# Inverse lengths by logarithm on ScalarE, unscaled maxima and value products in pieces in the first stage of an attention and maxout kernel

## The chip, the cores and the metric

The kernel runs on one core of one Trainium2 chip. A core has five engines that matter here: TensorE (matrix products, into PSUM), VectorE, ScalarE, GpSimd and SyncE (SP, which issues most of the transfers). Each engine works through its own instructions in the order in which the program gives them, and waits on semaphores for the others. The metric is the device time of one execution in microseconds; the kernel before takes 1111.87 us, the median of 3 runs (1109.64 to 1112.04).

## The reference

For 8 batches and 12 heads, queries and keys of 448 rows x 64 are divided by their root mean square and multiplied with gains; then softmax attention; the 12 heads' outputs of a row make a row of 768, which goes through three 768 x 768 layers, the largest of the three at each place, and a last 768 x 768 layer.

```python
def rmsnorm(x, g):
    rms = np.sqrt(np.mean(x * x, axis=-1, keepdims=True) + 1e-06)
    return x / rms * g
q_n, k_n = (rmsnorm(q, g_q), rmsnorm(k, g_k))
scores = np.matmul(q_n, k_n.transpose(0, 1, 3, 2)) / np.sqrt(64)
scores = scores - np.max(scores, axis=-1, keepdims=True)
attn = np.exp(scores)
attn = attn / (np.sum(attn, axis=-1, keepdims=True) + 1e-09)
attn_out = np.matmul(attn, v)
h = np.maximum(np.maximum(x @ w1, x @ w2), x @ w3)
out = h @ w_out
```

All inputs are float32. (The scale is written in one line here.)

## The kernel before

Two heads of a batch make a **pair**; there are 48 pairs, `g` = 0 to 47. Every pair is worked in 12 **beats** (`beat(g, i)`, `i` = 0 to 11), and a pair's 448 queries in four quarters `c` of 112, three beats each. The order of every engine is written out by hand: what a beat calls is recorded in the order of the calls, and `later(n, work)` puts work n beats on, to the end of that beat (`tick`). So an engine's order is the beats' order, and an engine can run ahead of another by some beats until it waits.

The work of one quarter: `scores` (TensorE), `row_max` (VectorE, the negative maximum, L550), `softmax` (ScalarE: L558 scales the maxima with `down`, L567 takes the exponential of `down * score + nm` for each of two heads). In the first six pairs (`PLAIN` = 6) scores and value products are float32 products; the exponentials `e` are transposed on TensorE (`turn_plain`), copied by ScalarE (`keep_turned`, L599, `pt`), and multiplied with the values in one go of eight products in beat 4 of the next pair (`add_values`, L680, into the only `av` buffer). The exponentials' sums are inverted, spread over the partitions (beat 5), copied (`keep_sums`, ScalarE, beat 6) and multiplied in (`scale_plain`, VectorE, beat 8); `finish` splits the result into two float16 parts `xt`: ScalarE the upper one in beat 9 (L705), VectorE the lower one a beat later (L706). From the seventh pair on everything is in two float16 parts and three products.

A pair's queries and keys are made ready two pairs ahead: squares (`squares`, GpSimd, L363; ScalarE for the first two pairs), their sums (VectorE, L370), mean and power -0.5 (`inv_rms`, GpSimd, L381 and L385, for keys and queries apart), scaling (`scale_k`, `scale_q`, GpSimd; VectorE for pair 0). In the plain pairs keys and queries are turned on TensorE (`turn_whole`, L461) and copied by ScalarE (`keep_whole`, L473 for keys, L475 for queries with the column of gains `gain_c`).

Beside the first pairs runs the preparation of the weights, in 24 blocks: a transfer (`raw`, L221, two buffers), ScalarE (L186), three decoding steps on VectorE (L194, L198, L203), a largest value over three blocks (L168), and then a split in two float16 parts: ScalarE L266 and L267, and GpSimd L270 for the lower part. The last one is called a weight piece below. From the seventh pair on the layers' products (L720, L784) fill TensorE between the attention's own, a few per beat (`thirds`).

The transfers of keys, queries, values and weights all stand in SP's one queue; a key load waits there until the scaling has freed its buffer.

## Time and profile before

| | |
|---|---|
| median of 3 runs | 1111.87 us (1109.64 to 1112.04) |
| the profiled execution | 1110.84 us; span of its records 1109.0 us |
| TensorE, VectorE, ScalarE, GpSimd busy | 1017.1, 755.3, 771.2, 702.4 us |
| mean granted TensorE clock | 0.967 |
| GpSimd's powers (L385) | 96 of 1603 ns, 153.9 us |
| scaling of the maxima (L558) | 192 of 265 ns, 50.9 us |
| exponentials (L567) of the plain pairs | 48 of 720 ns |

Busy time is that of an engine in all stages together; the plain pairs take the first 145 us or so, and in the rest TensorE is nearly full. A wait is told as the engine that idled, the line that it idled before, and the line that released it. In a timeline a row gives the start, the length, the engine, line, operation, what is written and read, and in brackets the idle time just before and what ended it.

### The profile page before, as it was taken

Reading aid. Unit: us, or ns where it says so; the run is one execution under the profiler, and the core shown is the slowest. Engines: PE = TensorE matmul, PEld = TensorE weight load, DVE = VectorE, ACT = ScalarE, POOL = GpSimd, SP = SyncE. Lnnn points to the kernel's source line nnn. Section 1 sums busy time; section 2 is a strip of 40 time slices with the busy share of each in tenths; the row PEclk is TensorE's granted clock in tenths of the full one; section 3 lists DMA queues with packets and bytes.
Section 4 is the critical chain, followed back from the end, with each engine's and each line's share of the span. In section 5 each row is a group of like instructions: output and inputs, shape, how many; then the busy total and the mean of one; then the engine's idle time right before and its main releaser. Section 6 shows DMA issues by size and latency. Waiting matters only on the chain. (4 is left out here: it accounts for less than half of the span.)

```text
span 1109.0 us, 18435 instructions
## 1 busy us (share of the span) xinstructions
PE 1017.1 (92%) x6184; PEld 500.3 (45%) x6184; DVE 755.3 (68%) x1397; ACT 771.2 (70%) x1767; POOL 702.4 (63%) x805
## 2 busy tenths in 40 slices
PE   4668759887899999999999999999999999999998
PEld 2334334343444444444444444444444444445554
DVE  4799988887667676776677766777677666662210
ACT  4599888767777687777777777777777777773001
POOL 5478888775767767677677675776767767610000
PEclk9697879998999999999999999999999999999999
DMA  5554567955888779777887798777877788564002
GB/s 150 161 164 151 139 175 142 188 118 102 172 147 147 134 153 179 152 142 139 170 149 143 143 164 173 144 137 154 169 142 139 140 173 154 91 106 87 1 1 57
DMA packets 426494, 152.30 MB, mean 137 GB/s; under 512 B 372896, under 2 KB 422048, under 8 KB 426400
## 3 DMA queue, kind: packets, MB, share of 16 engines
q1 hardware_dynamic: 425888, 150.95, 67.4%
q8 instruction: 49, 0.80, 0.3%
q14 instruction: 45, 0.37, 0.1%
q10 hardware_dynamic: 512, 0.18, 0.1%
HBM read 51.97 MB, written 11.01 MB: 57 GB/s over the span
## 5 line engine op out<-in xcount | busy, mean ns | idle before, releaser
L720 PE MATMUL acc<-xt,w_sb 128*128 128x448 f16 x2592 | 515.5, 354 | 2.7 <-DVE ht L744 2.2
L720 PEld LDWEIGHTS <-w_sb 128*128 128x128 f16 x2592 | 244.1, 98 | 260.8 <-issue 48.3
L550 DVE TENSOR_REDUCE sc<-sc 112x2 f32<-112x896 f32 x192 | 209.6, 1092 | 53.3 <-PE sc L541 52.2
L567 ACT ACTIVATE sc<-sc,nm,down 112x448 f32<-112x448 f32 x336 | 234.4, 698 | 11.2
L643 ACT ACTIVATE pp<-sc,rs 112x448 f16<-112x448 f32 x336 | 195.0, 633 | 52.0 <-ACT sc L567 47.4
L653 DVE SCALAR_TENSOR_TENSOR pp<-sc,rs,pp 112x448 f16<-112x448 f32 x336 | 212.9, 675 | 4.4 <-ACT pp L643 3.9
L784 PE MATMUL acc<-wo_sb,ht 128*128 128x384 f16 x864 | 151.9, 328 | 12.0 <-ACT osb L793 7.3
L558 ACT ACTIVATE nm<-sc,down 112x2 f32<-112x2 f32 x192 | 50.9, 265 | 158.2 <-DVE sc L550 157.7
L385 POOL TENSOR_TENSOR ri<-ri,half_neg 128x7 f32<-128x7 f32 x96 | 153.9, 1603 | 8.0
L541 PE MATMUL sc<-kt,qt 64*112 64x448 f16 x1008 | 132.1, 367 | 21.5 <-DVE pp L653 18.6
L749 POOL COPY hx<-ht 128x128 f16<-128x128 f16 x48 | 16.2, 337 | 168.0 <-DVE ht L744 167.6
L784 PEld LDWEIGHTS <-ht 128*128 128x128 f16 x864 | 81.4, 98 | 79.4 <-issue 29.0
L691 PE MATMUL av<-pt,vp 128*64 128x448 f16 x1008 | 109.9, 359 | 0.0
L541 PEld LDWEIGHTS <-qt 64*112 64x112 f16 x1008 | 54.2, 126 | 91.6 <-issue 52.4
L438 POOL TENSOR_TENSOR kp<-kn,kp 128x512 f16<-128x512 f32 x42 | 50.5, 1202 | 67.1 <-ACT kp L432 67.1
L636 DVE TENSOR_SCALAR rs<-sc 112x2 f32<-112x2 f32 x168 | 26.7, 159 | 91.1 <-ACT sc L567 91.0
L519 POOL TENSOR_TENSOR vp<-vr,vp 128x448 f16<-128x448 f32 x42 | 44.5, 1059 | 63.0 <-ACT vp L513 61.3
L691 PEld LDWEIGHTS <-vp 128*64 128x64 f16 x1008 | 50.1, 109 | 54.7 <-issue 29.5
L706 DVE SCALAR_TENSOR_TENSOR xt<-av,xt 128x448 f16<-128x448 f32 x42 | 26.2, 625 | 67.0 <-ACT xt L705 67.0
L370 DVE TENSOR_REDUCE ss<-sq 128x7 f32<-128x448 f32 x96 | 61.0, 637 | 10.4 <-ACT sq L361 6.4
L438 POOL TENSOR_TENSOR qp<-qn,qp 112x512 f16<-112x512 f32 x42 | 48.6, 1156 | 19.2 <-ACT qp L432 19.2
L505 POOL TENSOR_SCALAR vr<-vr,v_up 128x448 f32<-128x448 f32 x42 | 60.4, 1438 | 0.0
(111 smaller groups left out, 1202.6 us busy)
## 6 DMA issues: line engine op xcount, KB each, us to landing
raw<-in_moe_w_dram SPq DMA_DIRECT2D x18, 768.0 KB, 4.3
qr<-in_q_dram SPq DMA_DIRECT2D x48, 224.0 KB, 2.8
vr<-in_v_dram SPq DMA_DIRECT2D x96, 96.0 KB, 2.5
kr<-in_k_dram SPq DMA_DIRECT2D x95, 96.0 KB, 3.0
raw<-in_moe_w_out_dram SPq DMA_DIRECT2D x6, 768.0 KB, 5.1
pt<-pp SPq DMA_TRANSPOSE x168, 4.0
out_dram<-osb SPq DMA_DIRECT2D x8, 336.0 KB, 3.0
out_dram<-osb SPq DMA_DIRECT2D x8, 288.0 KB, 3.6
```

What stands on the lines that cost most here:

```text
L370: nc.vector.tensor_reduce(sums[g % 2][:sq.shape[0], KQ[what]], sq, axis=AX, op=ALU.add)
L385: nc.gpsimd.tensor_tensor(out=ri, in0=ri, in1=half_neg[:, at], op=ALU.pow)
L438: nc.gpsimd.tensor_tensor(out=parts[:, 1], in0=n, in1=parts[:, 0], op=ALU.subtract)
L505: nc.gpsimd.tensor_scalar(out=vr, in0=vr, scalar1=v_up[:, g // NP:g // NP + 1], scalar2=None, op0=ALU.mult,)
L541: nc.tensor.matmul(sc[:QP, h, :S], qt[rows, qp, c], kt[rows, kp, KEYS[h]], start=n == 0, stop=n == len(TERMS) - 1,)
L550: nc.vector.tensor_reduce(sc[:QP, 0, S + 8:S + 10], sc[:QP, :, :S], axis=AX, op=ALU.max, negate=True)
L567: nc.scalar.activation(to, sc[:QP, h, :S], AF.Exp, bias=nm[:, h:h + 1], scale=down[:QP], accum_out=total,)
L643: nc.scalar.activation(pp[:, 0, h], sc[:QP, h, :S], AF.Copy, scale=rs[:, h:h + 1])
L653: nc.vector.scalar_tensor_tensor(out=pp[:, 1, h], in0=sc[:QP, h, :S], scalar=rs[:, h:h + 1], in1=pp[:, 0, h], op0=ALU.mult, op1=ALU.subtract,)
L691: nc.tensor.matmul(av[half, :S], vp[rows, group, vpart], pt[rows, 7 * wp + group], start=u == 0 and n == 0, stop=u == 3 and n == len(TERMS ...
L720: nc.tensor.matmul(acc[:, :S], wt[:, wp, c], xs[c][:, xp], start=(c == 0 and n == 0), stop=(c == NCT - 1 and n == 2),)
L784: nc.tensor.matmul(acc[:, :HW], lhs, wo_sb[:, f, wp, half * HW:(half + 1) * HW], start=(f == 0 and n == 0), stop=(f == NFT - 1 and n == 2),)
```

## The change

Five things change.

- The power -0.5 of the mean squares is the exponential of -0.5 times the logarithm, two ScalarE operations on 128 x 15 for keys and queries together (`power`), followed by one Newton step (`newton`): four small GpSimd operations, three VectorE ones for the first two pairs. The mean is one operation (`mean_squares`, GpSimd; VectorE for the first two pairs). One table set for both functions is loaded at the start.
- The first pair's gains are worked later; `gain_c` holds the whole scale of the plain pairs' scores. So in the plain pairs `row_max` writes `nm` itself, and `softmax` has no scaling of the maxima there.
- Squares stand in beats 0 and 1 (before 0 and 3), their sums in 2 and 3 (before 2 and 5), the mean in 4, the power in 6, the Newton step and the keys' scaling in 8. Pair 1's scaling and turning are put later.
- For the first five pairs the value products come in four pieces in beats 2, 4, 5 and 7; spreading, copying and multiplying in of the sums in 8, 9 and 10 (before 5, 6, 8), `finish` in beat 11 (before 9).
- The order at the start is written anew: sums, mean and power for keys and queries together, then the keys, the gains' product, the queries.

```diff
+    nc.scalar.preload_act_table_set("natural_log_exp_and_others")
     nc.scalar.activation(warm, warm, AF.Exp)
...
-    def inv_rms(g, what):
...
-        nc.gpsimd.tensor_scalar(
-            out=ri, in0=sums[g % 2][:, at], scalar1=1.0 / D / QK_UP ** 2,
+    def mean_squares(g):
+        s = st[g]
+        s["ms"] = sb.tile([P, 15], F32, name="ms", bufs=2)
+        (nc.gpsimd if g > 1 else nc.vector).tensor_scalar(
+            out=s["ms"], in0=sums[g % 2], scalar1=1.0 / D / QK_UP ** 2,
             scalar2=RMS_EPS / QK_UP ** 2, op0=ALU.mult, op1=ALU.add,
         )
-        nc.gpsimd.tensor_tensor(out=ri, in0=ri, in1=half_neg[:, at], op=ALU.pow)
+    def power(g):
+        s = st[g]
+        ri = sb.tile([P, 15], F32, name="ri", bufs=2)
+        nc.scalar.activation(ri, s["ms"], AF.Ln)
+        nc.scalar.activation(ri, ri, AF.Exp, scale=-0.5)
+        s["ri"] = ri.rearrange("p (n o) -> p n o", o=1)
+    def newton(g):
+        s = st[g]
+        ms, ri = s.pop("ms"), s["ri"][:, :, 0]
+        t = sb.tile([P, 15], F32, name="newton", bufs=2)
+        if g > 1:
+            nc.gpsimd.tensor_tensor(out=t, in0=ms, in1=ri, op=ALU.mult)
+            nc.gpsimd.tensor_tensor(out=t, in0=t, in1=ri, op=ALU.mult)
+            nc.gpsimd.tensor_scalar(
+                out=t, in0=t, scalar1=-0.5, scalar2=1.5, op0=ALU.mult, op1=ALU.add
+            )
+            nc.gpsimd.tensor_tensor(out=ri, in0=ri, in1=t, op=ALU.mult)
+            return
...
     def row_max(g, c):
...
+        to = sc[:QP, 0, S + 8:S + 10]
+        if g < PLAIN:
+            to = s["nm", c] = sb.tile([QP, 2], F32, name="nm", bufs=3)
+        nc.vector.tensor_reduce(to, sc[:QP, :, :S], axis=AX, op=ALU.max, negate=True)
     def softmax(g, c):
...
-        nm = sb.tile([QP, 2], F32, name="nm", bufs=3)
-        nc.scalar.activation(nm, sc[:QP, 0, S + 8:S + 10], AF.Copy, scale=down[:QP])
         if g < PLAIN:
...
+            nm, by = s.pop(("nm", c)), 1.0
+        else:
+            nm, by = sb.tile([QP, 2], F32, name="nm", bufs=3), down[:QP]
+            nc.scalar.activation(nm, sc[:QP, 0, S + 8:S + 10], AF.Copy, scale=by)
...
-    sum_squares(0, "k")
-    inv_rms(0, "k")
-    sum_squares(0, "q")
-    inv_rms(0, "q")
-    prep_gain()
+        sum_squares(0, what)
+    mean_squares(0)
+    power(0)
+    newton(0)
     scale_k(0)
+    nc.vector.tensor_tensor(out=gain, in0=gains[:, 0], in1=gains[:, 1], op=ALU.mult)
     scale_q(0)
...
-    nc.scalar.copy(gain_c, column[:, 0:1])
+    nc.scalar.activation(
+        gain_c, column[:, 0:1], AF.Copy, scale=1.0 / QK_UP ** 2 / float(D) ** 0.5
+    )
...
-        inv_rms(1, what)
-    scale_k(1)
-    scale_q(1)
+    mean_squares(1)
+    later(0, lambda: power(1))
+    later(1, lambda: newton(1))
+    later(1, lambda: scale_k(1))
+    later(1, lambda: scale_q(1))
+    later(4, prep_gain)
...
-            if i == 5:
+            last = w == PLAIN - 1
+            if i == (5 if last else 8):
                 spread_sums(w)
-            if i == 6:
+            if i == (6 if last else 9):
                 keep_sums(w)
-            if i == (8 if w < PLAIN else 9):
+            if i == (8 if last else 10):
                 scale_plain(w)
-        if w >= 0 and i == (4 if w < PLAIN else 7):
+        if 0 <= w < PLAIN - 1 and i in (2, 4, 5, 7):
+            add_values(w, [(2, 4, 5, 7).index(i)])
+        elif w >= PLAIN - 1 and i == (4 if w < PLAIN else 7):
             add_values(w)
...
-        if w >= 0 and i == (9 if w < PLAIN else 10):
+        if w >= 0 and i == (11 if w < PLAIN - 1 else 9 if w < PLAIN else 10):
             finish(w, x_of[w // NP])
...
-                if i in (1, 4):
+                at = i - (1 if g else 4)
+                if at in (0, 3):
...
-            if i in (0, 3):
-                squares(n, "kq"[i // 3])
-            if i in (2, 5):
-                sum_squares(n, "kq"[i // 3])
-            if i in (5, 7):
-                inv_rms(n, "kq"[i // 7])
+            if i in (0, 1):
+                squares(n, "kq"[i])
+            if i in (2, 3):
+                sum_squares(n, "kq"[i - 2])
+            if i == 4:
+                mean_squares(n)
+            if i == 6:
+                power(n)
             if i == 8:
+                newton(n)
                 scale_k(n)
```

The lines of the changed kernel have other numbers, up to 30 apart. **VectorE, end of plain pair 2 and start of pair 3**, before: `xt` is the attention's lower part, the `sc` rows are the maxima, `w_sb` the decoding, `most` the largest of a block row.

```order
L706 SCALAR_TENSOR_TENSOR xt<-av,v_up,xt 128x448
L550 TENSOR_REDUCE sc<-sc 112x2
L194 TENSOR_SCALAR w_sb<-raw 128x768
L257 TENSOR_SCALAR w_most<-most 128x1
L260 RECIPROCAL w_up<-w_most 128x1
L261 TENSOR_SCALAR w_up<-w_up 128x1
L198 SCALAR_TENSOR_TENSOR w_sb<-raw,w_sb 128x768
L203 SCALAR_TENSOR_TENSOR w_sb<-raw,w_sb 128x768
L550 TENSOR_REDUCE sc<-sc 112x2
L611 RECIPROCAL sum<-sum 112x8
L370 TENSOR_REDUCE ss_84<-sq 128x7
L168 TENSOR_REDUCE most<-w_sb 128x1
```

The same place after:

```order
L256 TENSOR_SCALAR w_most<-most 128x1
L259 RECIPROCAL w_up<-w_most 128x1
L260 TENSOR_SCALAR w_up<-w_up 128x1
L735 SCALAR_TENSOR_TENSOR xt<-av,v_up,xt 128x448
L197 SCALAR_TENSOR_TENSOR w_sb<-raw,w_sb 128x768
L202 SCALAR_TENSOR_TENSOR w_sb<-raw,w_sb 128x768
L578 TENSOR_REDUCE nm<-sc 112x2
L639 RECIPROCAL sum<-sum 112x8
L369 TENSOR_REDUCE ss_83<-sq 128x7
L167 TENSOR_REDUCE most<-w_sb 128x1
L369 TENSOR_REDUCE ss_83<-sq 112x8
L193 TENSOR_SCALAR w_sb<-raw 128x768
```

`xt` has moved behind the next pair's first maximum and the first decoding step; the query sums (`ss`, 112x8) have moved from behind the third maximum to ahead of it.

**GpSimd, beats 0 to 8 of a plain pair**, before: `w_sb` is a weight piece, `sq` the query squares, `ri` the mean and the power for keys and then for queries.

```order
L270 TENSOR_TENSOR w_sb<-w_sb 128x768
L363 TENSOR_TENSOR sq<-qr 112x512
L270 TENSOR_TENSOR w_sb<-w_sb 128x768
L381 TENSOR_SCALAR ri<-ss_85 128x7
L385 TENSOR_TENSOR ri<-ri,half_neg 128x7
L381 TENSOR_SCALAR ri<-ss_85 128x8
L385 TENSOR_TENSOR ri<-ri,half_neg 128x8
```

After:

```order
L269 TENSOR_TENSOR w_sb<-w_sb 128x768
L362 TENSOR_TENSOR sq<-qr 112x512
L376 TENSOR_SCALAR ms<-ss_84 128x15
L269 TENSOR_TENSOR w_sb<-w_sb 128x768
L395 TENSOR_TENSOR newton<-ms,ri 128x15
L396 TENSOR_TENSOR newton<-newton,ri 128x15
L397 TENSOR_SCALAR newton<-newton 128x15
L400 TENSOR_TENSOR ri<-ri,newton 128x15
```

The mean now stands ahead of the second weight piece, and the Newton step behind it.

More of the change, by code (lines that the diff above doesn't have):

```diff
@@ L130, in qknorm_attention_maxout_ffn_kernel @@
     nc.vector.memset(warm, 0.0)
+    nc.scalar.preload_act_table_set("natural_log_exp_and_others")
     nc.scalar.activation(warm, warm, AF.Exp)
-    half_neg = const.tile([P, 15], F32, name="half_neg")
-    nc.vector.memset(half_neg, -0.5)
     sums = [const.tile([P, 15], F32, name=f"ss{i}") for i in range(2)]
@@ L666, in turn_weights, with add_values @@
         )
-    def add_values(g):
+    def add_values(g, groups=range(4)):
         s = st[g]
-        av = ps_a.tile([P, 512], F32, name="av", tag="a")
-        s["av"] = av
+        if "av" not in s:
+            s["av"] = ps_a.tile([P, 512], F32, name="av", tag="a")
+        av = s["av"]
         if g < PLAIN:
             vr, pt = s["vr"], pt_plain(s)
-            for u in range(4):
+            for u in groups:
                 for h, half in enumerate(HALVES):
@@ L853, in prep_gain @@
     def prep_gain():
-        nc.vector.tensor_tensor(out=gain, in0=gains[:, 0], in1=gains[:, 1], op=ALU.mult)
         row_largest(g_top[:, 0:1], gain)
@@ L883, in qknorm_attention_maxout_ffn_kernel @@
         )
-    nc.scalar.copy(gain_c, column[:, 0:1])
-    for what in "kq":
-        turn_whole(0, what)
+    turn_whole(0, "q")
+    nc.scalar.activation(
+        gain_c, column[:, 0:1], AF.Copy, scale=1.0 / QK_UP ** 2 / float(D) ** 0.5
+    )
     for what in "kq":
```

27 lines of the change are left out of this document (13 added, 14 removed).

## The prediction

> **What bounds the kernel now.** I read the busy time by stretches first, then the chain of waits, then the waits of the stretch that the change touches, then its timeline. In the stretches the columns are: window, its length, busy time of TensorE, its weight loads, VectorE, ScalarE and GpSimd, granted clock, DMA share, GB/s.
>
> ```profile
> 90.00:100.00 10.00, 7.13 (x52) 3.74 (x50) 8.79 (x13) 9.18 (x20) 7.85 (x8) 1.00 0.33 97
> ...
> 600.00:700.00 100.00, 97.47 (x627) 47.99 (x625) 69.96 (x139) 74.75 (x175) 71.46 (x86) 1.00 0.82 155
> ```
>
> There are two stages. In the plateau (600 to 700) TensorE is busy for 97.5 of 100 us and nothing else is above 75; its work is the same after the change. In the stage of the six plain pairs (90 to 100) TensorE is at 71%, ScalarE at 92%, VectorE at 88%. So what the plain stage gains or loses arrives at the end in full, and in the plateau only a new stall of TensorE counts. All but the plateau's part of the change lies in the first 165 us. The waits there (40 to 165 us; total, times, longest), asked of ScalarE alone:
>
> ```profile
> ACT qt L475 <- PE rows L461: 7.1, 3, 3.7
> ACT nm L558 <- DVE sc L550: 5.3, 5, 2.3
> ```
>
> ScalarE idles little, but VectorE is nearly as full, and the two wait for each other once a pair. That loop decides this case.
>
> **The start.** From the timeline (start, length, engine, line):
>
> ```profile
> 4.96 1.23 DVE L370 TENSOR_REDUCE ss<-sq 128x7 f32<-128x448 f32 x2 [3.91 <-ACT sq L361]
> ...
> 7.84 1.65 POOL L385 TENSOR_TENSOR ri<-ri,half_neg 128x8 f32<-128x8 f32 x1
> 8.21 0.23 DVE L854 TENSOR_TENSOR gain<-gains 128x64 f32<-128x64 f32 x1 [2.02 <-DMA gains<-in_g_k_dram]
> ...
> 12.42 0.64 ACT L475 ACTIVATE qt<-rows,gain_c 128x448 f32<-128x448 f32 x1 [0.22 <-PE rows L461]
> ...
> 14.99 1.10 DVE L550 TENSOR_REDUCE sc<-sc 112x2 f32<-112x896 f32 x1 [0.23 <-PE sc L533]
> ...
> 17.89 0.51 POOL L417 TENSOR_TENSOR kn<-kr,ri 128x192 f32<-128x192 f32 x1
> ...
> 19.51 0.81 SPq L340 DMA_DIRECT2D kr<-in_k_dram  x2
> ...
> 35.63 3.39 SPq L221 DMA_DIRECT2D raw<-in_moe_w_dram  x2
> ...
> 40.88 0.88 ACT L186 ACTIVATE raw<-raw 128x768 f32<-128x768 f32 x1 [3.63 <-DMA raw<-in_moe_w_dram]
> ```
>
> Before, the two powers on GpSimd end at 7.84 + 1.65 = 9.49. After, the sums end at 6.19; then one small VectorE operation, two ScalarE operations and three VectorE ones. Small ones of 128 x 1 to 128 x 64 take 0.15 to 0.25 us in this stretch (the gain product above: 0.23), so about 6 x 0.23 = 1.4 with their hand-overs: 7.6, that is 1.9 earlier. The gains' transfer (8.21) no longer stands ahead of the keys. So the first query tile (12.42) and the first maximum (14.99) come 1.9 earlier, at 13.1.
>
> For pair 1 the powers now wait behind the first exponentials: maximum to 14.2, exponentials to 15.7, logarithm and exponential 0.5, Newton step 0.6, then GpSimd's scaling of the keys, which takes 17.89 to 19.5 = 1.6 before: it ends at 18.5. That end releases SP's key load at 19.51, and behind it SP issues the value loads one after the other until the weight block at 35.63, whose landing ends ScalarE's wait of 3.63 at 40.88. So of 1.9 us only 19.5 - 18.5 = 0.95 passes this gate. Bounds: 0 (the block is late for another reason) and 1.9.
>
> **Pair 1 and the value products in four pieces.**
>
> ```profile
> 48.48 3.71 PE L680 MATMUL av<-pt,vr 128*64 128x448 f32 x16
> ...
> 52.77 0.64 ACT L475 ACTIVATE qt<-rows,gain_c 128x448 f32<-128x448 f32 x1 [3.73 <-PE rows L461]
> ```
>
> The query transposes stood behind all value products (3.71); now two of four pieces go ahead of them. But the first piece also stands ahead of the next scores and of the transposed weights that ScalarE copies before the query tile, so part of the 3.73 us comes back as a wait for those. I take 1.05 of it; bounds 0 and 3.7. Start and pair 1 together: -2.0, bounds 0 and -5.6.
>
> **Pairs 2 to 5: the loop.** Each pair's period is the distance of the first exponential (ScalarE):
>
> ```profile
> 61.73 0.73 ACT L567 ACTIVATE e<-sc,nm,down 112x448 f32<-112x448 f32 x1
> ...
> 81.88 0.72 ACT L567 ACTIVATE e<-sc,nm,down 112x448 f32<-112x448 f32 x1
> ...
> 92.33 0.73 ACT L567 ACTIVATE e<-sc,nm,down 112x448 f32<-112x448 f32 x1
> ...
> 102.26 0.26 ACT L558 ACTIVATE nm<-sc,down 112x2 f32<-112x2 f32 x1
> 102.55 0.72 ACT L567 ACTIVATE e<-sc,nm,down 112x448 f32<-112x448 f32 x1
> ...
> 112.93 0.64 ACT L475 ACTIVATE qt<-rows,gain_c 128x448 f32<-128x448 f32 x1 [2.50 <-PE rows L461]
> ...
> 124.77 0.72 ACT L567 ACTIVATE e<-sc,nm,down 112x448 f32<-112x448 f32 x1
> ...
> 145.41 0.70 ACT L567 ACTIVATE sc<-sc,nm,down 112x448 f32<-112x448 f32 x1
> ```
>
> Pairs 2 to 5 take 20.15, 20.67, 22.22 (with the 2.50 wait) and 20.64: 83.68. On ScalarE alone a pair would fall: four scalings of the maxima go (102.26 to 102.55, 0.29 each, 1.16), two small operations come (0.23 each, 0.46): -0.7, and the qt waits shrink. VectorE does not allow it:
>
> ```profile
> 95.57 0.94 DVE L198 SCALAR_TENSOR_TENSOR w_sb<-raw,w_sb 128x768 uint32<-128x768 uint32 x1
> ...
> 96.96 0.94 DVE L203 SCALAR_TENSOR_TENSOR w_sb<-raw,w_sb 128x768 uint32<-128x768 uint32 x1
> 99.08 0.68 DVE L706 SCALAR_TENSOR_TENSOR xt<-av,v_up,xt 128x448 f16<-128x448 f32 x1 [1.18 <-ACT xt L705]
> 99.68 1.09 DVE L550 TENSOR_REDUCE sc<-sc 112x2 f32<-112x896 f32 x1
> ...
> 101.60 1.34 DVE L198 SCALAR_TENSOR_TENSOR w_sb<-raw,w_sb 128x768 uint32<-128x768 uint32 x1
> 102.98 3.18 DVE L203 SCALAR_TENSOR_TENSOR w_sb<-raw,w_sb 128x768 uint32<-128x768 uint32 x1
> ...
> 107.68 2.54 DVE L168 TENSOR_REDUCE most<-w_sb 128x1 f32<-128x2304 f32 x1
> ...
> 111.59 1.09 DVE L550 TENSOR_REDUCE sc<-sc 112x2 f32<-112x896 f32 x1
> 112.59 0.68 DVE L370 TENSOR_REDUCE ss<-sq 112x8 f32<-112x512 f32 x1
> 113.19 0.95 DVE L203 SCALAR_TENSOR_TENSOR w_sb<-raw,w_sb 128x768 uint32<-128x768 uint32 x1
> ```
>
> Before, the loop is: VectorE's xt waits for ScalarE's (99.08, beat 9), runs on to the third quarter's maximum, which ends at 112.68 (13.6), and from the scaling of that maximum (0.3 ahead of the exponential at 92.33) to the next xt at 99.08 ScalarE needs 7.05: 20.65, the measured period. After, ScalarE's xt stands at beat 11, last ahead of the next pair's exponentials. ScalarE's side is then all from the third exponentials to the pair's end: 92.33 to 102.55 = 10.22, less two scalings (0.6), plus 0.46: 10.1. VectorE's side loses what now stands ahead of xt (99.68 to 101.60: 1.92) and gains the query sums, moved ahead of that maximum (112.59 to 113.19: 0.6): 13.6 - 1.92 + 0.6 = 12.3. In it lie 1.34 + 3.18 of decoding that take 0.94 each undisturbed: 2.6 of collision. So the period after is 10.1 + 12.3 - 2.6 = 19.8 plus the collisions c that are left. Before it is 20.67, so the point of decision is c = 0.85. The disturbers are GpSimd's:
>
> ```profile
> 102.09 1.64 POOL L363 TENSOR_TENSOR sq<-kr 128x448 f32<-128x448 f32 x1
> 103.70 1.65 POOL L270 TENSOR_TENSOR w_sb<-w_sb 128x768 f16<-128x768 f32 x1
> 105.31 1.75 POOL L363 TENSOR_TENSOR sq<-qr 112x512 f32<-112x512 f32 x1
> ```
>
> L203, ready at 102.98, ended at 106.16: it let two of them by. Without the powers (two of about 1.6 a pair) GpSimd is ahead: the key squares are done before xt, while the weight piece still starts with ScalarE's cast at the pair's end and the query squares follow it. Two decoding steps against these two cost 0.7 (VectorE goes first once) to 1.7 (they alternate); I take 1.7, as in the rows. A second place is new: GpSimd's one mean of squares waits for the query sums and holds back the next weight piece (beat 4), which before ran under the reduction at 107.68, whose 2.54 us no piece lengthened. Now it starts when VectorE decodes, just ahead of that maximum:
>
> ```profile
> 131.42 1.45 DVE L194 TENSOR_SCALAR w_sb<-raw 128x768 uint32<-128x768 uint32 x1
> 132.90 0.96 DVE L198 SCALAR_TENSOR_TENSOR w_sb<-raw,w_sb 128x768 uint32<-128x768 uint32 x1
> ```
>
> Where such a piece came first, L194 took 1.45; the step behind it, issued 0.03 us after its predecessor's end, was free (0.96). So 0 or the 1.65 of a piece; I take 0, since VectorE's next step is there first. With c = 1.7 pairs 3 to 5 take 21.5 each, 64.5 for 63.53: +1.0. Pair 2 has no weight piece at its start, c = 0.7, 20.5 for 20.15: +0.35. Sum of the loop +1.3; bounds -3.3 (c = 0.3 for all) and +8.
>
> The Trainium skill (SBUF — State Buffer, Who interferes with whom) says that of a VectorE and a GpSimd operation that both need the shared port pair the one that issues first keeps it for the whole instruction, while the other blocks fully. By that rule the weight piece of beat 4 loses to the decoding step, and the sum is the one above. The row of L203 at 102.98, which two GpSimd operations passed, differs from it; by that row the sum would be 6.6 us more.
>
> **The plateau.** Logarithm and exponential (0.46) come behind the third exponentials of each of 42 pairs. ScalarE idles just there, for VectorE's reciprocal, and again ahead of the next maxima:
>
> ```profile
> 600.32 1.16 ACT L643 ACTIVATE pp<-sc,rs 112x448 f16<-112x448 f32 x2 [0.48 <-ACT sc L567]
> ...
> 609.01 0.26 ACT L558 ACTIVATE nm<-sc,down 112x2 f32<-112x2 f32 x1 [1.25 <-DVE sc L550]
> ```
>
> GpSimd now scales after ScalarE's powers, about 2 us later than before in the pair; the value cast behind it may then wait up to 0.9, inside the 1.25. Hence 0; if that cover is gone, 0.46 x 42 = 19. Nothing waits for GpSimd's powers here, so their going gains nothing.
>
> **Sum.** -2.0 + 1.3 + 0 = -0.7. The profiled execution took 1110.84 (span 1109.0), 1.03 under the median of the runs, 1111.87: 1110.1 by the one, 1111.2 by the other. I say 1110.5, no change that can be measured: 0.2% or 2.2 us is about what tells from none.
>
> **Rivals.**
> 1. Faster: the collisions go with the powers (c = 0.3, the pairs at 20.1). Loop -3.3, start -2.0: 1105.5. For it: GpSimd, 79% busy from 90 to 100, loses 3.2 us a pair. Against it: its tensor operations, which collide, all stay. 30%.
> 2. Slower: the weight piece of beat 4 goes ahead of the decoding step, 1.65 in each of four pairs, +6.6 on my sum: 1117. It decides from c = 0.85 on. For it: the row at 102.98. Against it: VectorE's steps follow in 0.03. 22%.
> 3. Slower by ScalarE's logarithms in the plateau, up to 1129. Against it: the idle 0.48 in the same place. 5%.
>
> My own case has 43%. Most of it is no change. Faster 0.35, same 0.38, slower 0.27. The range 1105 to 1117 reaches from rival 1 to rival 2; my case alone would give 1107.5 to 1113.
>
> **What would show it.** The weight block's row on ScalarE near 39.9 instead of 40.88; the first exponential of pair 2 near 59.7 for 61.73; periods of 21 to 22 for pairs 3 to 5; VectorE's xt waiting for ScalarE's just ahead of each pair; long decoding rows right behind it. Periods under 20.5 prove rival 1, and decoding rows over 1.5 us just ahead of the third maximum rival 2. I am wrong altogether if TensorE's stalls in the plateau change by more than 3 us.

## The result, and the profile after

The changed kernel takes 1120.3 us (median of 4 runs, 1119.92 to 1123.27) beside 1111.95 us for the kernel before (4 runs); the ratio is 1.0084, 95% interval 1.0070 to 1.0097. It is slower by some 9 us, and above the predicted 1105 to 1117. The profiled execution took 1119.98 us, its span is 1118.1.

The stretches of the changed kernel (window, length, busy time of TensorE, weight loads, VectorE, ScalarE, GpSimd, granted clock, DMA share, GB/s):

```profile
90.00:100.00 10.00, 6.85 (x53) 3.98 (x54) 9.23 (x15) 8.13 (x19) 8.15 (x10) 1.00 0.43 140
600.00:700.00 100.00, 97.34 (x623) 47.76 (x621) 70.24 (x139) 76.69 (x189) 59.08 (x90) 1.00 0.84 156
```

In the plateau TensorE does in 100 us what it did before (97.34 for 97.47; from 300 to 1000 us the traces have 4314 products of each kernel), with GpSimd at 59 for 71. The loss lies ahead of it. ScalarE's timeline of the changed kernel shows the first exponential of pairs 2 to 6, the third quarter's exponential of pairs 4 and 5 (released by VectorE's maximum), and the value cast (`vp`) near the end of pairs 6 and 7:

```profile
58.45 0.63 ACT L595 ACTIVATE e<-sc,nm 112x448 f32<-112x448 f32 x1
...
79.74 0.63 ACT L595 ACTIVATE e<-sc,nm 112x448 f32<-112x448 f32 x1
...
102.39 0.62 ACT L595 ACTIVATE e<-sc,nm 112x448 f32<-112x448 f32 x1
...
114.25 0.63 ACT L595 ACTIVATE e<-sc,nm 112x448 f32<-112x448 f32 x1 [1.62 <-DVE nm L578]
...
125.04 0.62 ACT L595 ACTIVATE e<-sc,nm 112x448 f32<-112x448 f32 x1
...
139.37 0.63 ACT L595 ACTIVATE e<-sc,nm 112x448 f32<-112x448 f32 x1 [1.26 <-DVE nm L578]
...
150.44 0.70 ACT L595 ACTIVATE sc<-sc,nm,down 112x448 f32<-112x448 f32 x1
...
178.71 0.56 ACT L537 CAST vp<-vr 128x448 f16<-128x448 f32 x1 [0.22 <-POOL vr L529]
...
207.04 0.57 ACT L537 CAST vp<-vr 128x448 f16<-128x448 f32 x1
```

and of the kernel before, the same casts:

```profile
171.00 0.56 ACT L513 CAST vp<-vr 128x448 f16<-128x448 f32 x1
...
195.17 0.56 ACT L513 CAST vp<-vr 128x448 f16<-128x448 f32 x1
```

Pair 2 starts 3.3 us earlier than before (58.45 for 61.73); by pair 5 that is eaten up (125.04 for 124.77), at pair 6's first exponential the kernel is 5.0 late (150.44 for 145.41), at its cast 7.7, at pair 7's 11.9. From there to the end 2.8 come back: 9.1 at the end of the span.

The waits of the changed kernel in the window that the prediction read (40 to 165 us; total, times, longest):

```profile
ACT e L595 <- DVE nm L578: 9.1, 7, 2.5
...
ACT w_sb L266 <- POOL w_sb L269: 5.1, 4, 1.3
...
ACT qt L499 <- PE rows L485: 1.6, 2, 0.8
...
DVE xt L735 <- ACT xt L734: 9.9, 4, 2.5
...
POOL ms L376 <- DVE ss L369: 35.6, 6, 13.1
POOL newton L395 <- ACT ri L386: 9.9, 5, 4.5
```

The wait ahead of the query copy has gone as meant (7.1 before). VectorE's wait for xt was foretold, and so was GpSimd's for the query sums. Two that follow from it were not foretold here: GpSimd then waits for ScalarE's logarithm, and ScalarE's weight cast waits for GpSimd's weight piece. Pair 4 shows how they hang together, on GpSimd:

```profile
111.84 0.45 POOL L376 TENSOR_SCALAR ms<-ss 128x15 f32<-128x15 f32 x1 [5.55 <-DVE ss L369]
112.26 2.45 POOL L269 TENSOR_TENSOR w_sb<-w_sb 128x768 f16<-128x768 f32 x1
116.08 0.22 POOL L395 TENSOR_TENSOR newton<-ms,ri 128x15 f32<-128x15 f32 x1 [1.36 <-ACT ri L386]
116.38 1.77 POOL L396 TENSOR_TENSOR newton<-newton,ri 128x15 f32<-128x15 f32 x1
118.23 0.22 POOL L397 TENSOR_SCALAR newton<-newton 128x15 f32<-128x15 f32 x1
118.53 1.01 POOL L400 TENSOR_TENSOR ri<-ri,newton 128x15 f32<-128x15 f32 x1
...
121.28 2.46 POOL L269 TENSOR_TENSOR w_sb<-w_sb 128x768 f16<-128x768 f32 x1
```

and on ScalarE and VectorE at the end of that pair:

```profile
123.78 0.83 ACT L266 CAST w_sb<-w_sb 128x768 f16<-128x768 f32 x1 [1.27 <-POOL w_sb L269]
124.52 0.63 ACT L734 ACTIVATE xt<-av,v_up 128x448 f16<-128x448 f32 x1
...
125.18 0.69 DVE L735 SCALAR_TENSOR_TENSOR xt<-av,v_up,xt 128x448 f16<-128x448 f32 x1 [2.48 <-ACT xt L734]
125.78 4.62 DVE L197 SCALAR_TENSOR_TENSOR w_sb<-raw,w_sb 128x768 uint32<-128x768 uint32 x1
...
130.43 1.79 DVE L202 SCALAR_TENSOR_TENSOR w_sb<-raw,w_sb 128x768 uint32<-128x768 uint32 x1
```

GpSimd stands for 5.55 us, with a weight piece behind the waiting mean; then it waits 1.36 for the logarithm, and the Newton step runs from 116.08 to 119.54, 3.46 us for four operations on 15 columns. So the next weight piece ends at 123.74; ScalarE's cast, which overwrites what that piece reads, waits for it by 1.27 with xt and the next pair's exponentials behind it, and VectorE waits 2.48 for xt. The two decoding steps behind that wait take 4.62 and 1.79 us, where 0.94 each is the undisturbed time; behind the xt of pairs 2 and 3 they took 2.27 and 1.68.

### The profile page after: what moved, and what is told of

It is laid out like the page before. It is cut to its first block, busy times and chain, and to the rows that moved or that the text cites. A ratio compares the mean times of both kernels' runs of the same rounds, so it can differ in the third digit from the quotient of the medians.

```text
span 1118.1 us, 18596 instructions
## 1 busy us (share of the span) xinstructions
PE 1019.4 (91%) x6184; PEld 497.4 (44%) x6184; DVE 761.8 (68%) x1404; ACT 775.9 (69%) x1839; POOL 585.5 (52%) x843
## 5 line engine op out<-in xcount | busy, mean ns | idle before, releaser
L595 ACT ACTIVATE sc<-sc,nm,down 112x448 f32<-112x448 f32 x336 | 234.2, 697 | 11.2
L578 DVE TENSOR_REDUCE sc<-sc 112x2 f32<-112x896 f32 x168 | 183.5, 1092 | 65.3 <-PE sc L565 65.1
L590 ACT ACTIVATE nm<-sc,down 112x2 f32<-112x2 f32 x168 | 44.5, 265 | 137.7 <-DVE sc L578 137.4
L395 POOL TENSOR_TENSOR newton<-ms,ri 128x15 f32<-128x15 f32 x46 | 11.9, 258 | 166.2 <-ACT ri L386 166.2
```

What stands on the lines that cost most here:

```text
L578: nc.vector.tensor_reduce(to, sc[:QP, :, :S], axis=AX, op=ALU.max, negate=True)
L590: nc.scalar.activation(nm, sc[:QP, 0, S + 8:S + 10], AF.Copy, scale=by)
L595: nc.scalar.activation(to, sc[:QP, h, :S], AF.Exp, bias=nm[:, h:h + 1], scale=by, accum_out=total,)
```

## Experiments

All ratios are to the kernel before on the same chip, with a 95% interval. The profile of each run gives the places where the loss came up (first exponential of pairs 2 and 5, value cast of pairs 6 and 7, in us):

| run | pair 2 | pair 5 | cast 6 | cast 7 | median us | ratio |
|---|---|---|---|---|---|---|
| before | 61.73 | 124.77 | 171.00 | 195.17 | | 1 |
| changed kernel | 58.45 | 125.04 | 178.71 | 207.04 | 1120.3 | 1.0084 (1.0070-1.0097) |
| e1_whole | 60.48 | 123.44 | 173.54 | 201.86 | 1115.82 | 1.0037 (1.0023-1.0051) |
| e2_pieces | 58.71 | 121.49 | 172.38 | 196.53 | 1111.73 | 1.0003 (0.9994-1.0012) |
| e3_xt_behind | 58.58 | 123.24 | 175.69 | 204.01 | 1117.33 | 1.0047 (1.0034-1.0060) |
| e5_piece_ahead | 59.17 | 123.95 | 178.89 | 204.94 | 1117.14 | 1.0051 (1.0039-1.0064) |
| f2_pow_whole | 60.96 | 124.14 | 173.41 | 198.98 | 1111.4 | 0.9997 (0.9985-1.0009) |
| f3_pow | 57.22 | 118.93 | 168.52 | 192.77 | 1108.13 | 0.9972 (0.9963-0.9982) |
| f4_power_early | 60.11 | 126.35 | 178.97 | 204.53 | 1117.76 | 1.0055 (1.0043-1.0067) |
| f5_log_only | 60.48 | 125.61 | 175.71 | 203.79 | 1117.24 | 1.0054 (1.0042-1.0066) |
| g1_order_only | 58.99 | 119.81 | 169.03 | 192.96 | 1106.97 | 0.9966 (0.9954-0.9979) |
| g2_old_order | 58.72 | 127.73 | 182.07 | 209.84 | 1142.96 | 1.0293 (1.0279-1.0307) |
| g4_cures | 59.02 | 118.10 | 171.07 | 197.58 | 1110.16 | 0.9994 (0.9985-1.0003) |
| g3_pow_xt_behind | 58.20 | 117.57 | 165.16 | 189.32 | 1104.72 | 0.9947 (0.9934-0.9959) |
| h2_no_newton | 59.39 | 121.90 | 174.24 | 198.63 | 1111.05 | 1.0005 (0.9996-1.0014) |
| h4_log_late | 58.55 | 118.90 | 166.50 | 190.75 | 1104.67 | 0.9944 (0.9932-0.9957) |
| h1_order_xt | 58.23 | 117.39 | 163.90 | 188.02 | 1101.4 | 0.9922 (0.9908-0.9936) |
| i1_newton_vector | 58.59 | 122.50 | 173.79 | 198.70 | 1114.32 | 1.0029 (1.0017-1.0041) |
| i2_newton_vector_xt | 59.26 | 120.92 | 169.81 | 194.70 | 1110.64 | 0.9992 (0.9983-1.0000) |

The places are those of one execution each. f2's took 1114.27 us, 2.9 over its median, and the runs that have the start and the pieces of the change reach pair 2 anywhere from 57.22 to 60.11, so that differences of 1 or 2 us in the place of pair 2 say little.

### Is it the pieces and the late end of a pair?

My first theory (A) was the prediction's own: xt in beat 11 and the decoding bunched behind VectorE's wait for it. Four runs:

e1_whole:

```diff
-            if i == (5 if last else 8):
+            if i == 5:
                 spread_sums(w)
...
-        if 0 <= w < PLAIN - 1 and i in (2, 4, 5, 7):
-            add_values(w, [(2, 4, 5, 7).index(i)])
-        elif w >= PLAIN - 1 and i == (4 if w < PLAIN else 7):
+        if w >= 0 and i == (4 if w < PLAIN else 7):
             add_values(w)
```

> The changed kernel with the value products of the first six pairs issued whole again at beat 4, and the sums, scaling and xt at their beats of before (5, 6, 8, 9); the logarithm, the unscaled maxima and the start stay. Theory A (the late end of the four pieces: ScalarE's xt in beat 11, VectorE waiting 2.48 us a pair for it, and the decoding steps bunched behind that wait, where they meet GpSimd): the wait of VectorE's xt goes, the four periods of pairs 2 to 5 come back from 92.0 us to 82-85, the gain of the start (3.3 us at the first exponential of pair 2) stays, and the time is 1106-1110 us, faster than both. Theory B (ScalarE's weight cast waits 1.27 us a pair for GpSimd's weight piece, which the Newton step has made late): the pieces have no part in it, periods of 90-92 us, 1117-1121. Theory C (moved query sums and logarithm load VectorE and ScalarE): as B, 1116-1121.

e2_pieces is the reverse on the kernel before: the same lines, put in.

> The kernel before with the four pieces and the late beats of the changed kernel (pieces at 2, 4, 5, 7; sums 8 and 9, scaling 10, xt 11 for pairs 0 to 4) and nothing else: powers by GpSimd, scaled maxima and the old start stay. Theory A: slower than before by the 8 us of the loop and what runs on into pairs 6 and 7: 1119-1126 us, with VectorE's xt waiting over 2 us ahead of each pair. Theory B (weight piece late by the Newton step): the Newton step isn't there, so the cast isn't late, and the pieces cost at most 3 us: 1111-1115. Theory C: within 2 us of before, 1110-1114.

e3_xt_behind:

```diff
         later(1, lambda: nc.vector.scalar_tensor_tensor(
             out=xt[:, 1], in0=av[:, :S], scalar=by, in1=xt[:, 0],
             op0=ALU.mult, op1=ALU.subtract,
-        ))
+        ), g < PLAIN - 1)
```

> The changed kernel with VectorE's xt of pairs 0 to 4 issued one decoding step later (behind the shift step of the decoding, no longer ahead of it), so that the step runs while ScalarE's xt is being made. Theory A, as far as it is VectorE's wait: the 2.48 us a pair that VectorE stands idle are filled by a step of 0.9 us or more, 1 us a pair and over comes back, periods of 86-89 us instead of 92.0 and 1113-1117 us. If it is the bunched decoding against GpSimd and not the wait: the step runs longer where it stands, 1117-1121. Theory B: ScalarE's chain sets the end, no change, 1119-1121.

e5_piece_ahead:

```diff
-                later(4 + 4 * j, lambda n=n, f=f: lower(n, f), True)
+                later((4, 7, 12)[j], lambda n=n, f=f: lower(n, f), True)
```

> The changed kernel with the second of the three weight pieces of a row on GpSimd issued one beat earlier, ahead of the Newton step and the key scaling instead of behind them. Theory B: ScalarE's weight cast in beat 10 no longer waits (1.27 us, four times), xt and with it the next pair come that much earlier: periods of 87 us instead of 92.0, 1114-1116 us. Theory A: ScalarE's wait for the cast is a part only, since VectorE still waits for an xt in beat 11 and the decoding behind it still meets GpSimd: 1117-1120.

Theory A fell. The pieces and late beats alone leave the time of the kernel before (1.0003), and the changed kernel without them is still 0.37% slower. Pieces and the rest together cost 0.84%, more than both apart, so something in the rest makes the pieces dear. But inside e2 two things cancel: pair 2 starts 3.0 us earlier, and pairs 2 to 5 take 86.41 us for 83.68, all of it in pair 5, where the decoding step behind xt takes 4.29. Theories B and C hit e2 (1111.7 in 1111-1115 and 1110-1114), but missed e1, which came out between A's range and theirs (1115.8). e3 (1117.3) and e5 (1117.1) stayed just above the bounds of the theories that they were made for, A's 1117 and B's 1116. e3 (1.0047 for 1.0084) and e5 (1.0051) each gave back some 0.35%: both waits that they aim at are real. In e5 the cast's wait is nearly gone, here of that run from 58 to 146 us:

```profile
ACT w_sb L266 <- POOL w_sb L269: 1.0, 3, 0.4
```

### Powers or start?

Theory D: the new way of taking the powers, which all of e1, e3 and e5 still have. f2_pow_whole and f3_pow take it out from pair 2 on (f2 with whole products, f3 with the pieces), f5_log_only puts it alone into the kernel before, and f4_power_early moves ScalarE's part one beat ahead. The edit of f3 (without the lines that bring `inv_rms` back):

```diff
-            if i in (0, 1):
-                squares(n, "kq"[i])
-            if i in (2, 3):
-                sum_squares(n, "kq"[i - 2])
-            if i == 4:
-                mean_squares(n)
-            if i == 6:
-                power(n)
+            if i in (0, 3):
+                squares(n, "kq"[i // 3])
+            if i in (2, 5):
+                sum_squares(n, "kq"[i // 3])
+            if i in (5, 7):
+                inv_rms(n, "kq"[i // 7])
             if i == 8:
-                newton(n)
                 scale_k(n)
```

> The changed kernel with two parts undone: from pair 2 on the powers are taken by GpSimd as before (squares at beats 0 and 3, sums at 2 and 5, mean and power at 5 and 7, no logarithm, no Newton step), and the value products are whole at their old beats. The start of the change and the unscaled maxima of the first six pairs stay. Theory D (what is lost is lost by the new order of GpSimd's work: mean, weight piece, a wait of 1.4 to 5.7 us for ScalarE's logarithm, then Newton step, keys, weight piece, queries, squares without a break, under which a decoding step stands 4 us): without it the gain of the start and of the quicker exponentials is left, first exponential of pair 5 at 121-124 us, pair 7's value cast by 196 us, total 1107-1111. Theory E (the new start or the unscaled maxima push the first pairs to where they collide): as the run with whole products, 1114-1117.

> The changed kernel with GpSimd's powers of before from pair 2 on, as in the run above; pieces, late beats, unscaled maxima and the new start stay. Theory D: the pieces alone have cost nothing on the kernel before (ratio 1.0003), so that without the new order of GpSimd 1107-1112 us, faster than the changed kernel by 8 or more. Theory E: the powers have no part, 1117-1121. If pieces and powers each cost by themselves what they cost together: 1115-1117.

f4:

```diff
-            if i == 6:
+            if i == 5:
                 power(n)
```

> The changed kernel with ScalarE's logarithm and exponential of the powers one beat earlier (beat 5, ahead of the quarter's exponentials at beat 6 and not behind them), all else the same. Theory D, as far as it is GpSimd's wait for ScalarE: the Newton step waits some 4 us less in pairs 6 and 7 and over 1 us less in pairs 2 to 5, GpSimd's run ends that much earlier, and 3 to 6 us come back: 1114-1117 us. If it is the mere order on GpSimd and not the wait, or theory E: 1119-1122, or slower where ScalarE now waits for the mean.

f5 is the reverse of f3's edit on the kernel before, with the table set loaded at the start.

> The kernel before with the powers of the change alone from pair 2 on (squares at 0 and 1, sums at 2 and 3, mean at 4, logarithm at 6, Newton step at 8) and its table of functions loaded at the start; old start, scaled maxima, whole products. Theory D: slower than before by 4-8 us, 1115-1119, with the loss between pair 5 and pair 7's value cast. Theory E: 1110-1113, no difference.

Theory D holds, though f2 missed its upper bound by 0.4 us and f4 by 0.8. The powers alone make the kernel before 0.54% slower (6.0 us). Without them the rest of the change is faster than before, 0.9972; with them it is 1.0084, so that on top of the rest they cost about 12.5 us (1.0084 - 0.9972 of 1111). And the pieces have two signs: with GpSimd's powers they gain (0.9972 for f2's 0.9997), with logarithms they lose (1.0084 for e1's 1.0037). The waits point to a reason. In f3 from 58 to 146 us

```profile
DVE xt L751 <- ACT xt L750: 2.9, 4, 0.7
...
POOL ri L420 <- DVE ss L372: 10.8, 4, 3.3
POOL w_sb L272 <- ACT w_sb L269: 5.9, 3, 3.3
```

there is no cast waiting for a weight piece: GpSimd waits for ScalarE's cast, not the other way round, and VectorE waits for xt by 0.7 at most. With xt as ScalarE's last work of a pair, whatever makes the cast ahead of it late goes straight into the period. With xt at beat 9 less of it does: from pair 2 to pair 5 e1 takes 62.96 us and before 63.04 (f5 65.13, the changed kernel 66.59); what e1 loses, it loses from pair 5 to pair 7's cast. That the late cast is what turns the pieces' sign is argued, not shown: in e5, which has the pieces and hardly any of that wait, the time is still 1.0051, above e1's 1.0037.

f4 (1.0055) gave back 0.3%, all of it between pairs 6 and 7: from cast to cast 25.56 us, where the changed kernel and e1 took 28.3 and the kernel before 24.17. What is lost there in the changed kernel are these rows, of GpSimd, VectorE and ScalarE:

```profile
169.95 0.22 POOL L395 TENSOR_TENSOR newton<-ms,ri 128x15 f32<-128x15 f32 x1 [5.65 <-ACT ri L386]
...
179.96 4.02 DVE L197 SCALAR_TENSOR_TENSOR wo_sb<-raw,wo_sb 128x768 uint32<-128x768 uint32 x1
183.90 0.15 DVE L664 TENSOR_SCALAR rs<-sc 112x2 f32<-112x2 f32 x1
...
184.61 1.16 ACT L671 ACTIVATE pp<-sc,rs 112x448 f16<-112x448 f32 x2 [3.06 <-issue]
```

GpSimd, held 5.65 us by the logarithm, then works without a break from 169.95 to 184.99 (keys, weight piece, queries, values, squares). A decoding step issued at 179.96 under that run takes 4.02; the sums' reciprocal stands behind it, and ScalarE's product with that reciprocal comes after 3.06 us of idling (for which the profile names no releaser). In h2_no_newton (below) GpSimd had a break of 0.64 us there, and the same step took 0.95:

```profile
174.83 0.95 DVE L197 SCALAR_TENSOR_TENSOR wo_sb<-raw,wo_sb 128x768 uint32<-128x768 uint32 x1
...
174.88 1.79 POOL L543 TENSOR_TENSOR vp<-vr,vp 128x448 f16<-128x448 f32 x1 [0.64 <-ACT vp L537]
```

In f4, which keeps the Newton step and only has the logarithm earlier, the break is there too, and the step took 1.45:

```profile
179.61 1.03 POOL L543 TENSOR_TENSOR vp<-vr,vp 128x448 f16<-128x448 f32 x1 [0.64 <-ACT vp L537]
...
180.00 1.45 DVE L197 SCALAR_TENSOR_TENSOR wo_sb<-raw,wo_sb 128x768 uint32<-128x768 uint32 x1
```

So between casts 6 and 7 the rows point not to the length of the four operations (0.22 us each, 169.95 to 171.07), but to GpSimd's work, which, begun late, has no break where the decoding step comes.

### Which part of the powers?

D1: the order of squares and sums. D2: the round from GpSimd to ScalarE and back, with the Newton step. g1_order_only puts only the order (squares 0 and 1, sums 2 and 3) into f3; g2_old_order puts the old order into the changed kernel:

```diff
-            if i in (0, 1):
-                squares(n, "kq"[i])
-            if i in (2, 3):
-                sum_squares(n, "kq"[i - 2])
-            if i == 4:
+            if i in (0, 3):
+                squares(n, "kq"[i // 3])
+            if i in (2, 5):
+                sum_squares(n, "kq"[i // 3])
+            if i == 6:
                 mean_squares(n)
-            if i == 6:
+            if i == 7:
                 power(n)
```

> The run with GpSimd's powers, pieces, new start and unscaled maxima (ratio 0.9972), and on top of it only the order of the change for the squares and their sums (squares at beats 0 and 1, sums at 2 and 3; GpSimd still takes mean and power at 5 and 7, no logarithm). Theory D1 (the order costs: two squares in a row on GpSimd at the pair's begin, 0.6 us of sums ahead of VectorE's third maximum): most of the 12 us between the changed kernel and that run come back as a loss, 1115-1120. Theory D2 (the round GpSimd - ScalarE - GpSimd of mean, logarithm and Newton step costs, with what stands behind it): the order alone costs at most 2 us, 1107-1110.

> The changed kernel with the squares and sums at their old beats (0 and 3, 2 and 5) and the mean at beat 6, the logarithm at 7, the Newton step at 8 as it was: the weight piece of beat 4 then stands ahead of the mean on GpSimd, and the query sums behind the third maximum on VectorE. Theory D1: 1108-1112, nearly all of the loss gone. Theory D2: GpSimd still waits for ScalarE's logarithm and its run still ends late: 1116-1121.

> The changed kernel with three cures at once: ScalarE's logarithm at beat 5, GpSimd's first two weight pieces one beat earlier (ahead of the mean and of the Newton step), VectorE's xt behind the decoding step. Singly they gave back 2.5, 3.2 and 3.0 us. Theory D (all three waits belong to GpSimd's late run and to ScalarE's and VectorE's waits for it): 1110-1114, most of the loss. If they are three names of one wait: 1116-1118, no better than each.

> The run with GpSimd's powers, pieces, new start and unscaled maxima, and VectorE's xt behind the decoding step. VectorE's wait for ScalarE's xt is 0.7 us a pair there and not 2.48, so that at most 0.7 us for each of four pairs can come back: 1105.5-1108.5 us.

D1 fell: the order alone costs nothing (0.9966 for 0.9972). g2 missed both numbers. The later the round begins, the worse: 22.7 us over the changed kernel, of which 2.8 are there by pair 7's cast (209.84 for 207.04) and the rest is a new stall in each pair of the plateau. Its stretch and its wait (the second from 300 to 1000 us) in g2:

```profile
600.00:700.00 100.00, 93.94 (x601) 46.21 (x600) 68.93 (x137) 74.42 (x181) 56.73 (x88) 1.00 0.79 147
...
ACT vp L537 <- POOL vr L529: 63.3, 34, 3.0
```

and the same wait in the changed kernel:

```profile
ACT vp L537 <- POOL vr L529: 8.5, 7, 1.6
```

GpSimd's scaling of the values stands behind the Newton step and the keys; two beats later it is what ScalarE waits for, and TensorE falls from 97.3 to 93.9. The changed kernel was close to that edge. g4 (0.9994) took back 0.9% with three small moves, about the sum of what f4, e5 and e3 gave one by one (0.29, 0.33 and 0.37%; g4 also has the first piece a beat earlier). g3 was below its bound by 0.8 us, on a chip whose kernel before is 0.4 faster: xt behind the decoding gives 0.25% also where the wait is 0.7 a pair.

The last runs ask which half of the round it is, the wait or the four operations. h2_no_newton leaves `newton(n)` out from pair 2 on; h4_log_late is g3 with the logarithm from pair 10 on; h1_order_xt is g1 with xt behind the decoding.

> The changed kernel without the Newton step of the pairs from 2 on (GpSimd's four small instructions on 15 columns are left out, and the power is the bare result of logarithm and exponential); GpSimd's mean, ScalarE's logarithm and the wait between them stay. Theory D2a (the detour over ScalarE costs: GpSimd waits for the logarithm whatever it does with it): at most the 3.2 us that the four took at 116 come back from each of four pairs in part, 1117-1121. Theory D2b (the four instructions cost, 0.22 us each where nothing disturbs them and up to 1.77 beside VectorE): 2-3 us a pair, 1109-1114.

> The run with GpSimd's powers, pieces, new start, unscaled maxima and xt behind the decoding (ratio 0.9947), with the logarithm, its order and its Newton step from pair 10 on, where the weights are prepared, and GpSimd's powers before. If the logarithm costs only in pairs 2 to 9 and is hidden behind TensorE afterwards: 1104-1106, the same as that run. If it costs in each pair: 1107-1113.

> The run with GpSimd's powers, pieces, new start and unscaled maxima (0.9972) with both edits that gave something: the order of the change for squares and sums (0.9966) and xt behind the decoding (0.9947). If they act in different places: 1103-1105. If the 1 us of the order and the wait for xt are the same wait: 1104.5-1107.

Without the Newton step the changed kernel takes the time of the kernel before (1.0005): D2b, the Newton step. That is 8.8 of the 12.5 us that the new way of the powers cost on top of the rest; the 3.7 that are left (1.0005 for f3's 0.9972) lie in the other half of the round, the detour over ScalarE, and no run takes them apart further. Of the 8.8, 4.1 come back from pair 2 to pair 5 (62.51 us for 66.59) and 3.9 from cast 6 to cast 7 (24.39 for 28.33). How they differ from stage to stage shows in the changed kernel's groups of the Newton tile (count; least, median and longest ns; first and last start), first in the plain pairs, then in the plateau:

```profile
L396 POOL TENSOR_TENSOR newton<-newton,ri x4: 1755/1763/1783, 71.1 to 141.5; 128x15 f32<-128x15 f32 x4
...
L396 POOL TENSOR_TENSOR newton<-newton,ri x34: 218/219/222, 313.1 to 969.0; 128x15 f32<-128x15 f32 x34
```

Eight times as long, in each of pairs 2 to 5 (in pairs 0 and 1 it took 0.22). The wait between the mean and the keys stays in h2 (5.2 us in four pairs), but no wait of the cast for a weight piece is left from 40 to 165 us, and VectorE's for xt is 1.3 at most (58 to 146 us):

```profile
DVE xt L735 <- ACT xt L734: 5.2, 4, 1.3
...
POOL kn L440 <- ACT ri L386: 5.2, 4, 1.3
```

At the end of pair 4 in h2, ScalarE's cast comes without a wait, and the decoding step behind xt is nearly as long as with the Newton step (4.62):

```profile
120.64 0.83 ACT L266 CAST w_sb<-w_sb 128x768 f16<-128x768 f32 x1
...
121.90 0.62 ACT L595 ACTIVATE e<-sc,nm 112x448 f32<-112x448 f32 x1
...
122.64 4.19 DVE L197 SCALAR_TENSOR_TENSOR w_sb<-raw,w_sb 128x768 uint32<-128x768 uint32 x1
```

h4 is g3's time (0.9944 for 0.9947): in the plateau, at the beats of the change, the logarithm and its Newton step cost nothing and gain nothing. h1 (0.9922, 1101.4 us), below both of its expected ranges, is the fastest here and beats both kernels: start, unscaled maxima, pieces, the new order, GpSimd's powers, and xt behind the decoding.

Since h2 leaves work out, the step's place was asked for by itself: three VectorE operations in place of GpSimd's four.

```diff
-        if g > 1:
+        if g < 0:
             nc.gpsimd.tensor_tensor(out=t, in0=ms, in1=ri, op=ALU.mult)
```

> The changed kernel with the Newton step of the pairs from 2 on made by VectorE (three small operations, as for the first two pairs) and not by GpSimd; logarithm, pieces, order and late beats stay, and the result is again the full one. If it is GpSimd's four instructions beside VectorE's decoding that cost (3.5 us of GpSimd's time a pair, and what waits for the weight piece behind them): three operations of some 0.2 us on VectorE, ahead of the decoding step, cost 0.6 us a pair, so that the run without the Newton step (1.0005) is nearly reached: 1111-1114 us. If leaving the step out had gained only by what else it moved: 1116-1120.

> The same with VectorE's xt behind the decoding step, which gave 3.0 us on the changed kernel and 3.4 on the one with GpSimd's powers: 1108-1111 us if the two act in different places, and so faster than before with logarithms; 1111-1114 if the wait for xt has gone with the Newton step.

i1 took back 0.55% of h2's 0.79%, a little less than expected. The three operations take 0.15 to 0.18 us each in pairs 2 to 5, but GpSimd's keys now wait up to 3.1 us for them. So the step's place is the larger part; some 2.7 us between h2 and i1 remain with the step on VectorE, that wait among them. i2 (0.9992) shows xt's wait to be another loss than the Newton step's. With logarithms in the plain pairs nothing here was faster than before by more than 0.2%; with GpSimd's powers there, five runs were.

## Why the prediction was wrong

**The start and pair 1 (-2.0).** Right in sign, too small: -3.3 at pair 2. The split was wrong. ScalarE's row of the weight block came at 40.43, 0.45 earlier and not 0.95 (the working's own 19.5 - 18.5 would be 1.0). Start and unscaled maxima without pieces gain 0.8 at pair 2 (f2: 60.96), the pieces without them 3.0 (e2: 58.71), both 4.5 (f3: 57.22); with the scatter of single executions (57.22 to 60.11) this is rough, but the larger part lies with the pieces. Pair 1's wait of 3.73 us for its query copy fell to 0.85, where I had let only 1.05 of it pass.

**The loop (+1.3, bounds -3.3 and +8).** This step failed. Pairs 2 to 5 took 91.99 for 83.68: +8.3, just past the bound, and 7.0 over the 85.0 that I had added up. The failing sentence is "Without the powers (two of about 1.6 a pair) GpSimd is ahead". I took the two powers off GpSimd and never put on what came in their place: the way over ScalarE, and the Newton step, four operations on GpSimd, which I had priced (0.6 us) for pair 1 alone. The mean's wait for the query sums I did see, with the weight piece behind it, but followed it to VectorE's decoding and no further. From the query sums on, GpSimd needed 9.5 us to the last key (111.7 to 121.2), with a weight piece among it. The term left out is the cast behind it: 1.27 us in each of four pairs, and through xt in beat 11 into the next pair. h2 gives the size of the omission: without the Newton step the loop takes 86.31, 1.3 over my sum.

The two sides of my working show where the 7.0 lie. ScalarE's side, from the third quarter's exponentials to the pair's end, was to be 10.1; it took 10.8 in pairs 2 to 4 and 11.1 in pair 5, 3.0 too much in all, and without the Newton step 9.6 and 9.9 (h2). VectorE's side, 9.7 plus the collisions c, took 10.5, 11.9, 11.9 and 14.3: so c was 0.8, 2.2 and 2.2, near the 0.7 and 1.7 that I had put there, but 4.6 in pair 5. Of that side's miss of 4.0 us pair 5 alone has 2.9. This term was mis-sized: the two decoding steps behind xt took 4.62 and 1.79 there, 4.5 over the undisturbed 1.9. One of them is as long without the Newton step (4.19 in h2), with the pieces alone (4.29 in e2) and with the new powers alone (4.39 in f5), so this loss is another than the Newton step's. Why they are longer in pair 5 than in pairs 3 and 4 (2.27 and 1.68) was not tried.

What the loop's working said of the two collisions was half right. Decoding behind xt was long (4.62 behind pair 4's), and the decoding ahead of the third maximum stayed undisturbed while the weight piece of beat 4 took 2.45, as I had chosen; rival 2 did not happen. All decoding rows from 58 to 150 us together lengthened no more than before: by 11.2 us over their undisturbed 0.55 and 0.94 in the changed kernel, by 12.6 in the kernel before (sums over 36 and 40 rows). So it matters which row is long, and what stands behind it. The Trainium skill's rule that I weighed there (SBUF — State Buffer, Who interferes with whom) fits the 2.45, and does not fit the 4.62: three GpSimd operations that issued after that decoding step passed it. In the row that I had set against the rule (L203 at 102.98), one of the two that I counted had begun first, at 102.09, so that only one passed.

**Pairs 6 and 7 were not in the sum.** I had closed it at the last plain pair, though the weights' preparation goes on to pair 9. From pair 6's first exponential (+5.0) to pair 7's cast (+11.9) another 6.8 us went: 56.60 for 49.76. The same cause has about half of it: h2, without the Newton step, takes 52.93 there, f3, with GpSimd's powers, 51.14.

**The plateau (0).** Right: h4 shows it apart. The value cast's wait for GpSimd, for which I had allowed 0.9, came and was longer (up to 1.6, in seven pairs from 300 to 1000 us); g2, where it comes in 34 pairs, shows how little cover was left.

**The rivals.** Rival 1 (faster, 1105.5) is nearly what the rest of the change does without its powers (1108.1). I had given it 30% for a reason that was backwards: that the powers go. The result's sign was rival 2's, by another mechanism.

**What I had not counted at all:** the exponentials of the plain pairs became 0.09 us shorter each (last section).

## What to carry to other kernels

When an operation is taken off an engine, list what that engine does in its place, with its own waits, before calling it relieved: here less busy time (585.5 for 702.4 us on GpSimd) came with later results. An in-order engine that waits holds back everything queued behind it, so price a new wait by who needs the work behind it, and look for a reader whose buffer another engine is about to overwrite. And before moving an engine's last work of a round to the round's very end, ask what stands ahead of it there: the same four pieces were worth -2.8 us with GpSimd's powers, +0.3 on the kernel before, and +5.2 with the logarithm and the Newton step.

## What the runs showed of the hardware

Small operations on GpSimd are not small beside VectorE's decoding. The Newton step's second operation took 0.22 us in the plateau and 1.76 in each of pairs 2 to 5, the fourth 0.22 and 1.01; in pair 4 both end within 0.1 us of a decoding step's end (VectorE's L197 to 118.06, L202 to 119.46):

```profile
117.12 0.94 DVE L197 SCALAR_TENSOR_TENSOR w_sb<-raw,w_sb 128x768 uint32<-128x768 uint32 x1
...
118.52 0.94 DVE L202 SCALAR_TENSOR_TENSOR w_sb<-raw,w_sb 128x768 uint32<-128x768 uint32 x1
```

What holds them was not tried by itself; the second one's record begins 0.74 us before that decoding step's. Three VectorE operations for the same step took 0.15 to 0.18 each in pairs 2 to 5, and 0.17 in the median of all (i1).

A pointer for the scale costs ScalarE time. The groups of the plain pairs' exponentials from 58 to 120 us (busy us, mean ns), of the kernel before:

```profile
L567 ACT ACTIVATE e<-sc,nm,down 112x448 f32<-112x448 f32 x25 | 17.9, 720 | 0.4
```

and of the changed kernel, where the scale is a constant 1:

```profile
L595 ACT ACTIVATE e<-sc,nm 112x448 f32<-112x448 f32 x24 | 15.0, 633 | 5.4 <-DVE nm L578 5.4
```

87 ns less for each. The Trainium skill (ScalarE: Activation LUTs, What ACT_TABLE_LOAD costs) says that each pointer operand of [128,1] adds about 93 ns; with a pointer over 112 partitions the rows agree within 6 ns.
